# A planned two-MLP attention kernel: four feature tiles of every batch ahead of the other twelve, in new engine orders

## The chip, the core and the metric

The kernel runs on one core of one Trainium2 chip. The metric is the device time of one execution in microseconds (us), the median of three runs. The core's engines are TensorE (PE in the profile; PEld is its weight load), VectorE (DVE), ScalarE (ACT), GpSimd (POOL) and SyncE (SP), whose queue issues nearly all DMA transfers here.

## The reference

Three stages, all in float32. `q`, `k`, `v` have 4 batches of 8 heads, 576 rows, 64 columns.

```python
# Nystrom attention, per batch and head; m = 32 landmarks, each a mean of 18 rows
q_lm, k_lm = q.reshape(B, H, 32, 18, D).mean(3), k.reshape(B, H, 32, 18, D).mean(3)
A, Bm, C = sm(q, k_lm), sm(q_lm, k_lm), sm(q_lm, k)        # sm: softmax of scale * a @ b.T
Z = Bm.T / (norm1(Bm) * norminf(Bm) + 1e-6)
for _ in range(6):
    Z = 2 * Z - Z @ Bm @ Z
x = A @ Z @ C @ v                                          # then (2304, 512)
h = x @ w_in;  x = (h * cos(h)) @ w_out                    # first MLP, 2048 features
h = x @ w_in2; out = (max(h, 0) + alpha * min(h, 0)) @ w_out2   # second MLP
```

The four weights arrive as float64 and are read as pairs of 32-bit words.

## The kernel before

**Products in three passes.** Each operand of a large matmul is split into a rounded part and a rest (`split`, `sub` at L410, the ACT copy at L552 and L1055), and a product is three matmuls: high by high, high by low, low by high.

**Units.** The attention of one batch is two units of four heads (`unit`, L624). The units of batch 0 are u0 and u1 in the order's names, those of batches 1 to 3 are U2 to U7. A unit loads k, q and v (L638, L649, L665), transposes k and q on PE, forms the landmark means (for batches 0 and 1 on PE, L720; for batches 2 and 3 by a tree of additions on POOL, L742), makes the scores (L766), the softmax of C, C by v (L816), and the softmax of A, whose transpose is split into high and low tiles. 

**z path.** `z_path` (L863) runs the iteration for Z. It begins with the products of L882, goes through some fifteen short DVE steps and then through seven products (L936), each waiting for a DVE step (L953) on the one before. Its last product (L965) gives the small matrix `wt`. z0 belongs to batch 0, z1 to batch 1, and z2 to batches 2 and 3 together, in tiles of double width. Only z0 has fillers between its products: matmuls without use, in pairs, named w (L533); ten more pairs open the program.

**V'.** `vprime` (L976) multiplies `wt` by four tiles of the first MLP's input weights (L999, 16 matmul records for 512 features) and splits the result on ACT (L1004) and DVE (L1006). So the first MLP's input product takes A as its moving operand and V' as its weights.

**Ticks.** A tick (`tick`, L1027) is one feature tile of 128 features for one half batch of 288 rows: six matmuls make h (L1043), then ACT, DVE, ACT, DVE, ACT and POOL or DVE form h cos h and split it, and four groups of three matmuls (y, L1068) add it into four PSUM banks. The y groups of a tick stand in PE's order some ticks after its h. There are 128 ticks: first feature tiles 0 to 7 of batches 0 and 1, then 8 to 15 of these, then all 16 of batch 2 and of batch 3. At the end of a block of feature tiles (`e` in the order) the four banks are copied out and stored in `y1d`; a second block of the same half batch reads `y1d` and adds (L1088).

**Weights.** `convert` (L557) loads 512 KB of float64 weights into one of three `raw` tiles (L562) and makes float32 of it by three DVE steps (L568, L570, L572). c0 to c31 are the first MLP's: for each group of 512 features four input tiles, which are also spilled to `w1d` for later batches, and four output tiles. Batches 2 and 3 read their input weights from `w1d` (L983). c32 to c55 are the second MLP's.

**Second MLP.** It is a Strassen product of seven matmul groups (L1357), with the output product at L1438, and runs after the last tick. Its weights and activations take tiles that the first MLP gives up; `place` gives every tag its addresses and an age, and a tile may lie over older ones.

**What sets the order.** `ORDER` is a text of all operations by name, such as `t12:1` (h of tick 12) or `u0:41/V` (the 41st operation of u0, on DVE), and `go` (L327) issues them in that order, each to its engine's in-order queue; without a letter an operation goes to the first engine it names. Due times and `after` lists served a planner that wrote the text; at run time only data dependencies and buffers make an engine wait.

Of the kernel before, what the change touches and what calls it, by code (L numbers as in the profile page):

```python
# [10 lines left out]
F32R = mybir.dt.float32r  # L11
# [21 lines left out]
t3:1 c5:2 U3:16/V t2:4 t1:6 U3:15/A v1:1 t3:2 t0:9 t0:10 t0:8 t2:5 c5:3 t1:7/V c5:4 t3:3 U2:27 t2:6 v1:2 v1:3 U3:10
t0:11 c0:5 c8:5 c1:5 c7:1 c5:5 v1:4 c5:6/V t3:4 U3:11/A U3:12/A v1:5 c6:2 t3:5 U2:28 c12:2 c6:3 t1:9 t4:1 t1:11 U2:23
t5:1 t3:6 t4:2 U2:24/A U2:25/A c6:4 c12:3 t2:7/V t4:3 U2:26 t1:8 t1:10 c6:5 t5:2 t4:4 c6:6/G t5:3 U2:29 U2:30 t4:5
c12:4 t3:7/V t5:4 t4:6 t4:7/G t6:1 t5:5 U2:31 c7:2 U2:32 t7:1 t6:2 t7:2 t5:6 U3:4 U3:5/A t2:9 t2:10 z1:1 t2:8 c7:3
c7:4 U2:33 U2:34/G t7:3 z1:2 z1:3 t6:3 c13:1 c14:1 c9:5 U3:3 c15:1 U3:6/A c7:5 t7:4 t6:4 t5:7/G c7:6/G U3:17 t2:11
U2:35 t7:5 t6:5 U3:19 U3:18 c13:2 U3:20 c13:3 U3:21 U3:22 t8:1 t3:9 t3:10 t3:8 t3:11 t8:2 t6:6 z1:4 t7:6 U2:36 U3:27
U2:37 U3:23 t7:7/G t6:7/G t9:1 c13:4 U2:38 t8:3 z1:5 U3:24/A U3:25/A t8:4 U3:26 z1:6 U2:39/V U3:28 U2:40 z1:7 U3:29
z1:8 U3:7 U2:41 t8:5 z1:9 c12:5 t10:1 U2:42/V U3:8/A c13:5 t9:2 U3:9/A c12:6/V t4:10 z1:17 t4:11 t4:9 t4:8 c14:2  # L40
z1:10 c14:3 t9:3 c13:6/V z1:11 c14:4 t5:9 t5:10 t5:11 t5:8 t9:4 t10:2 t8:6 c14:5 t8:7/G t9:5 z1:12 t10:3 c14:6/V
t11:1 t10:4 t9:6 t9:7/G t11:2 c15:2 z1:13 t10:5 t11:3 z1:14 t6:9 t6:10 t6:11 t12:1 t6:8 t11:4 c15:3 z1:15 t11:5 c15:4
z1:16 t13:1 z1:18 c15:5 t13:2 t12:2 t10:6 U3:30 c15:6/V t13:3 z1:19 U3:31 U3:32 U3:33 t10:7/G U3:34/G t7:8 t7:9 t7:11
z1:20 t7:10 t13:4 t12:3 z1:21 e7:2/A e7:1/A t12:4 e7:4/A U3:35 t11:6 t11:7/G t8:11 z1:22 t12:5 e7:5/V z1:23 e7:3
# [301 lines left out]
def kernel(  # L346
# [1170 lines left out]
```

## Time and profile before

| | us |
|---|---|
| median of three runs | 829.88 |
| lowest and highest | 827.96, 831.62 |
| span of the profiled execution | 827.8 |
| PE busy | 805.2 |
| DVE busy | 610.1 |
| ACT busy | 419.4 |
| POOL busy | 192.9 |

The page gives the profiled execution's span alone; its own time beside it is not shown. In this document a stretch of the trace is bounded by marks of the order: the start of the first h matmul (L1043) of a tick. Tick 0 is at 46.9 us, tick 24 at 128.1, tick 40 at 172.3, tick 64 at 268.1 and tick 127, the last, at 431.1. A gap in which PE stands idle is length less busy time; short waits between pipelined matmuls hide in the busy time.

### The profile page before, as it was taken

What the parts mean: (1) busy time and instruction counts of PE and PEld (TensorE: products, weight loads), DVE (VectorE), ACT (ScalarE), POOL (GpSimd) and SP (SyncE); (2) the same over time, 40 slices, a digit from 0 to 9 for tenths busy, and PEclk for the clock granted to TensorE, in tenths of its full rate; (3) what the DMA queues carried; (4) which work ended last, traced back from release to release, by engine and by line L of the source; (5) the groups of instructions that cost most, each with busy time, mean ns of one, the idle gap of its engine ahead of it and who ended that gap; (6) DMA issues with size and microseconds to landing.
All of it is one profiled execution on the core that took longest, in us unless ns stands there. A gap on an engine that the chain in (4) does not pass through costs nothing.

```text
span 827.8 us, 16875 instructions
## 1 busy us (share of the span) xinstructions
PE 805.2 (97%) x6490; PEld 717.1 (87%) x6490; DVE 610.1 (74%) x1256; ACT 419.4 (51%) x943; POOL 192.9 (23%) x217
## 2 busy tenths in 40 slices
PE   8889999999999999999999999999999999999997
PEld 6567789988788898899999888989998989999886
DVE  3999799877886867889788998765565556456653
ACT  4468655778754557567764444522433244323231
POOL 0003312435530112036621113203400133000020
PEclk9999999999999999999999999999999999999999
DMA  9985466675666864454542422221031012120231
GB/s 222 217 236 155 132 164 209 164 173 115 137 206 210 259 199 151 146 181 168 168 146 87 131 90 66 78 85 39 13 102 51 9 57 83 48 62 14 81 111 26
DMA packets 87904, 103.34 MB, mean 125 GB/s; under 512 B 35856, under 2 KB 62992, under 8 KB 87824
## 3 DMA queue, kind: packets, MB, share of 16 engines
q1 hardware_dynamic: 87744, 102.14, 43.0%
q8 instruction: 51, 0.84, 0.4%
q14 instruction: 29, 0.24, 0.1%
q10 hardware_dynamic: 80, 0.13, 0.0%
HBM read 79.96 MB, written 22.28 MB: 124 GB/s over the span
## 4 chain that ended last, share of the span: by engine, by line
PE 70%; DVE 16%; ACT 5%; DMA 4%; issue 3%; POOL 0%; SPq 0%; DVEq 0%; ACTq 0%; POOLq 0%
PE acc L1438 20%; PE acc L1068 16%; PE h L1357 10%; PE h L1043 8%; PE x L1357 7%; DVE m L410 3%; DVE m L1050 1%; PE x L999 1%; DMA m<-in_moe_w_in_dram 1%; DVE m L572 1%; DVE m L570 1%; DVE m L1053 1%; DMA m<-wi2d 1%; PE x L1402 1%; PE h L1402 1%
## 5 line engine op out<-in xcount | busy, mean ns | idle before, releaser
L410 POOL TENSOR_TENSOR m<-m,m 128x288 fp32r<-128x288 f32 (+4 forms) x154 | 147.1, 968 | 580.0 <-ACT m L1055 213.5
L1068 PE MATMUL acc<-m,m 128*128 128x288 f32 x1536 | 235.4, 299 | 0.1
L1068 PEld LDWEIGHTS acc<-m,m 128*128 128x128 f32 x1536 | 211.2, 188 | 18.7 <-issue 12.7
L1438 PE MATMUL acc<-m,m 128*128 128x512 f32 x864 | 218.0, 392 | 0.6 <-ACT m L1426 0.2
L410 DVE TENSOR_TENSOR m<-m,m 128x512 fp32r<-128x512 f32 (+4 forms) x246 | 151.5, 636 | 48.3 <-ACT m L1426 18.1
L1438 PEld LDWEIGHTS acc<-m,m 128*128 128x128 f32 x864 | 154.1, 188 | 28.4 <-DVE m L410 1.3
L1043 PE MATMUL h<-m,m 128*128 128x288 f32 x768 | 125.0, 302 | 2.5 <-DVE m L1053 1.5
L1043 PEld LDWEIGHTS h<-m,m 128*128 128x128 f32 x768 | 108.5, 190 | 8.3 <-DVE m L1053 4.6
L1357 PE MATMUL h<-m,m 128*128 128x256 f32 x768 | 108.5, 282 | 0.3 <-ACT m L405 0.2
L1357 PEld LDWEIGHTS h<-m,m 128*128 128x128 f32 x768 | 102.6, 189 | 6.3 <-ACT m L405 0.7
L1426 ACT ACTIVATE m<-m 128x512 fp32r<-128x512 f32 (+1 forms) x80 | 46.1, 585 | 92.0 <-DVE m L1424 87.4
L1052 ACT ACTIVATE m<-m,quarter 128x288 f32<-128x288 f32 x128 | 67.0, 533 | 34.5 <-DVE m L1050 33.6
L1357 PE MATMUL x<-m,m 128*128 128x256 f32 x576 | 81.7, 283 | 0.3 <-DVE m L407 0.3
L1357 PEld LDWEIGHTS x<-m,m 128*128 128x128 f32 x576 | 76.5, 189 | 4.2 <-DVE m L407 0.6
L1048 ACT ACTIVATE m<-h 128x288 int32<-128x288 f32 x128 | 51.4, 406 | 47.3 <-PE h L1043 46.4
L405 ACT ACTIVATE m<-h 128x256 f32<-128x256 f32 (+2 forms) x86 | 33.5, 392 | 81.8 <-PE h L1357 65.0
L1050 DVE SCALAR_TENSOR_TENSOR m<-h,m 128x288 f32<-128x288 f32 x128 | 57.0, 450 | 23.8 <-ACT m L1048 23.4
L1055 ACT ACTIVATE m<-m 128x288 fp32r<-128x288 f32 x128 | 55.7, 440 | 30.5 <-DVE m L1053 25.6
L1053 DVE TENSOR_TENSOR m<-m,h 128x288 f32<-128x288 f32 x128 | 56.9, 448 | 12.9 <-ACT m L1052 10.1
L1189 ACT ACTIVATE m<-m 128x512 fp32r<-128x512 f32 x68 | 41.6, 625 | 29.2 <-PE h L1357 10.5
L1380 DVE TENSOR_TENSOR m<-h,m 128x512 f32<-128x512 f32 x32 | 21.9, 686 | 32.8 <-ACT m L405 21.8
L1424 DVE SCALAR_TENSOR_TENSOR m<-m,m 128x512 f32<-128x512 f32 x64 | 45.0, 718 | 0.8
(147 smaller groups left out, 768.0 us busy)
## 6 DMA issues: line engine op xcount, KB each, us to landing
m<-in_moe_w_in_dram SPq DMA_DIRECT2D x32, 512.0 KB, 5.6
m<-wi2d SPq DMA_DIRECT2D x56, 256.0 KB, 3.0
m<-in_moe_w_out_dram SPq DMA_DIRECT2D x24, 512.0 KB, 5.2
m<-w1d SPq DMA_DIRECT2D x32, 256.0 KB, 5.4
y1d<-m SPq DMA_DIRECT2D x24, 288.0 KB, 4.4
out_dram<-m SPq DMA_DIRECT2D x35, 128.0 KB, 2.8
w1d<-m SPq DMA_DIRECT2D x16, 256.0 KB, 5.6
wi2d<-m SPq DMA_DIRECT2D x16, 256.0 KB, 3.2
```

Of the source, the lines that this page charges most:

```text
L410: ENG[e].tensor_tensor(o, a, b, op=ALU.subtract)
L1043: nc.tensor.matmul(out=hp.t[:, 0:CW], lhsT=w_[:, js], rhs=x[:, cs], start=(i == 0), stop=(i == 5))
L1048: op(act(CW, True), lambda e: nc.scalar.activation(k_.t, hp.t[:, 0:CW], AF.Copy, scale=INV2PI, bias=0.25), r=[hp], w=[k_], target=T + 0.8)
L1050: op(dve(CW), lambda e: nc.vector.scalar_tensor_tensor(u.t, hp.t[:, 0:CW], INV2PI, k_.t, op0=ALU.mult, op1=ALU.subtract), r=[hp, k_], w=[u])
L1052: op(act(CW), lambda e: nc.scalar.activation(u.t, u.t, AF.Sin, scale=2.0 * math.pi, bias=quarter), rw=[u], aset="sin")
L1053: op(dve(CW), lambda e: nc.vector.tensor_tensor(hc.t, u.t, hp.t[:, 0:CW], op=ALU.mult), r=[hp, u], w=[hc], target=T + 2.6)
L1055: op(act(CW), lambda e: nc.scalar.activation(gh.t, hc.t, AF.Copy), r=[hc], w=[gh, gl])
L1068: nc.tensor.matmul(out=yg[o].t[:, 0:CW], lhsT=w_.t[:, sl], rhs=x.t, start=(j == ja and i == 0), stop=(j == jb and i == 2),)
L1357: nc.tensor.matmul(out=rv(k), lhsT=a_.t[:, p, c2, js], rhs=b_.t[:, q_, c2, 0:hw], start=(first and c2 == 0 and i == 0), stop=(c2 == 1 and ...
L1424: op(dve(w), lambda e, m_=m_, hv=hv: nc.vector.scalar_tensor_tensor(m_.t[:, 0:w], hv(), 0.0, m_.t[:, 0:w], op0=ALU.max, op1=ALU.add), r=hr ...
L1426: op(act(w), lambda e, m_=m_, gh=gh: nc.scalar.activation(gh.t[:, 0:w], m_.t[:, 0:w], AF.Copy), r=[m_], w=[gh, gl])
L1438: nc.tensor.matmul(out=ya[n][t].t, lhsT=gv(x_), rhs=r_.t, start=(st and k == 0), stop=(en and k == 2))
```

## The change

1. The 128 ticks come in another sequence: feature tiles 0 to 3 of batches 0, 1, 2, 3, then tiles 4 to 15 of each batch. There are 16 blocks in place of 12, and every second block reads `y1d` back.
2. Batches 2 and 3 get a z path each, z2 and z3, in single width.
3. V' of the first 512 features takes the input tiles in place for all four batches (no spill of these); later groups of batches 1 to 3 read `w1d`: 36 reads in place of 32, 12 spills in place of 16.
4. k and q are loaded by transfers over 128 partitions (two heads of 64 groups of nine rows, one above the other) in place of 64; heads take other places in the tiles, and later products follow suit.
5. A tiles of batches 2 and 3, and half of the V' tiles, move to other addresses (`a2`, `a3`, `vb`, `wq`).
6. `ORDER` is new throughout.

```diff
-KN = dict(T0=46, TA=3.4, TBT=3.05, VE=4.0, U1=-1, U2=30, U3=42, UA=88, UD=7, UZ=17, C2=48, CD=3.0, LA=4, JG=8, VG=8, LW=4, LG=4)
+KN = dict(T0=40, TA=3.2, TBT=2.55, VE=4.0, C2=40, CD=3.2, LA=4, VG=10, LW=4, LG=4)
+BLOCKS = [(b, 0, 4) for b in range(4)] + [(b, 4, 16) for b in range(4)]
...
-    at = lay(0, 0, ("f", 4, 4 * FW), ("wo", 8, 2048))
-    at_va = at
+    at_wo = lay(0, 0, ("f", 4, 4 * FW))
+    at_va = lay(0, at_wo, ("wo", 8, 2048))
+    lay(1, at_wo, ("vb", 4, 4096))
+    at = lay(2, at_wo, ("wq", 8, 2048))
...
-    at_1 = lay(1, at_w, ("wp", 24, 2048), ("vb", 4, 4096))
+    at_1 = at_vb + 16384
+    lay(1, at_w, ("wp", 24, 2048), ("a2", 7, 4 * S))
...
+    place["a3"] = (1.5, 4 * S, [z0 + 12288])
...
     def conv_wi(fb, p):
         def done(cf):
             wi1[fb, p] = cf
-            spill((fb, p), w1, w1d[p, :, fb * 512:fb * 512 + 512])(cf)
+            if fb:
+                spill((fb, p), w1, w1d[p, :, fb * 512:fb * 512 + 512])(cf)
...
-                    for bb in range(2):
+                    for hh in range(2):
                         nc.sync.dma_start(
-                            out=t.t[64 * bb:64 * bb + 64].rearrange("p (h x) -> p h x", h=2),
-                            in_=src[b, 4 * c + 2 * bb:4 * c + 2 * bb + 2].rearrange("h (p r) d -> p h (r d)", r=NR),
+                            out=t.t[:, hh * NR * D:(hh + 1) * NR * D],
+                            in_=src[b, 4 * c + 2 * hh:4 * c + 2 * hh + 2].rearrange("b (p r) d -> (b p) (r d)", r=NR),
                         )
...
-                o = loads(4, ld, 3.28, w=[t], after=aft)
+                o = loads(2, ld, 3.28, w=[t], after=aft)
...
-        ah[b, c] = (sb("a", [P, S], F32R), sb("a", [P, S], F32R))
+        ah[b, c] = tuple(sb(("a" if b < 2 else "a3" if b + c + i == 5 else "a2"), [P, S], F32R) for i in range(2))
...
     def vprime(b, fb, target):
-        if b > 1:
+        if b and fb:
...
-    ticks = [(b, ch, j) for jg in range(0, NF, JG) for b in range(2) for ch in range(2) for j in range(jg, jg + JG)]
-    ticks += [(b, ch, j) for b in range(2, NB) for ch in range(2) for j in range(NF)]
+    ticks = [(b, ch, j, ja, jb - 1) for b, ja, jb in BLOCKS for ch in range(2) for j in range(ja, jb)]
...
-        if b != 2:
-            z_path([b] if b < 2 else [2, 3], tick_time(s + KN["UZ"]))
-            gates["v"] = [g.ops[-1]]
+        z_path([b], tick_time(t - 2))
+        gates["v"] = [g.ops[-1]]
...
```

Counted in the two texts of `ORDER`, between the same marks. PE operations of units and z are counted as the order names them; those of the joint z2 are of double size.

| | h | y groups | V' | of units | of z | conversion steps on DVE |
|---|---|---|---|---|---|---|
| before, to tick 0 | 0 | 0 | 1 | 33 | 9 | 19 |
| before, tick 0 to 24 | 24 | 80 | 3 | 13 | 9 | 52 |
| before, tick 24 to 40 | 16 | 64 | 3 | 3 | 0 | 25 |
| before, tick 40 to 64 | 24 | 100 | 2 | 24 | 9 (double) | 15 |
| before, after tick 64 | 64 | 268 | 7 | 1 | 0 | 57 |
| new, to tick 0 | 0 | 0 | 1 | 35 | 10 | 18 |
| new, tick 0 to 24 | 24 | 90 | 3 | 39 | 26 | 20 |
| new, tick 24 to 64 | 40 | 153 | 6 | 0 | 0 | 80 |
| new, after tick 64 | 64 | 269 | 6 | 0 | 0 | 50 |

The order of SP to the first V' was k and q of u0, c3, k and q of u1, c0, v of u0 and u1, c2, c1, then k and q of U2 and more conversions. It becomes k and q of u0, c4, k and q of u1, c2, c3, c1, k and q of U2, v of u0 and u1, q and k of U3, c0, c5, v of U2, c7, c6. Between ticks 24 and 44 the new order issues 18 conversion loads, 9 spills, 7 transfers of `y1d` and 4 reads of `w1d`. The exponent and the sine need different tables on ACT: the order before changes between them 20 times, the new one 12 times, 11 of these before tick 24.

## Rows read from the trace of the kernel before

**Rows 1.** The page: span, and TensorE's busy time and instructions.
```profile
span 827.8 us, 16875 instructions
...
PE 805.2 (97%) x6490; PEld 717.1 (87%) x6490; DVE 610.1 (74%) x1256; ACT 419.4 (51%) x943; POOL 192.9 (23%) x217
```

**Rows 2.** Windows, six stretches between marks (columns in the first line).
```profile
core 0: us, PE busy (x) PEld busy (x) DVE busy (x) ACT busy (x) POOL busy (x), PEclk, DMA share, GB/s
0.00:46.90 46.90, 37.29 (x587) 26.08 (x587) 30.19 (x85) 19.99 (x43) 3.11 (x11) 0.99 0.95 216
46.90:128.10 81.20, 77.16 (x790) 65.56 (x790) 73.22 (x174) 54.39 (x121) 19.35 (x20) 0.98 0.59 170
128.10:172.30 44.20, 44.20 (x355) 40.88 (x355) 39.81 (x78) 30.91 (x73) 18.58 (x20) 1.00 0.70 190
172.30:268.10 95.80, 92.72 (x1056) 79.33 (x1055) 74.90 (x188) 64.53 (x140) 33.13 (x45) 1.00 0.65 166
268.10:431.10 163.00, 162.47 (x1257) 152.88 (x1255) 131.06 (x269) 105.05 (x246) 51.00 (x54) 1.00 0.55 181
431.10:827.90 396.80, 391.36 (x2454) 352.34 (x2454) 260.92 (x467) 144.50 (x321) 67.68 (x68) 1.00 0.21 65
```

**Rows 3.** Chain of waits near 300 us: start, length, what, how many.
```profile
295.46 3.58 PE acc L1068 x27
...
299.04 1.02 PE x L999 x16
...
303.04 1.59 PE h L1043 x12
```

**Rows 4.** Timeline of PE, z path products: one of z0, then z2's.
```profile
38.10 0.43 PE L936 MATMUL h<-m 32*32 32x64 f32 x16 [0.48 <-DVE m L953]
...
235.36 0.46 PE L882 MATMUL x<-m 64*32 64x32 f32 x32
...
255.26 0.87 PE L936 MATMUL x<-m 32*32 32x96 f32 x32
...
259.05 0.67 PE L965 MATMUL x<-m 32*64 32x32 f32 x32
```

**Rows 5.** Timeline of PE: the first V' product.
```profile
41.33 1.33 PE L999 MATMUL x<-m,m 64*32 64x512 f32 x16 [0.60 <-ACT m L731]
```

**Rows 6.** Chain of waits before the first tick: conversion steps, V' copies, tick step.
```profile
19.45 0.43 DVE m L568
...
31.55 0.60 DVE m L570
...
42.68 0.61 ACT m L1004
...
43.31 0.69 DVE m L1006
...
49.83 0.37 DVE m L1050
```

**Rows 7.** Windows before v0 and where transfers are dense (columns as above).
```profile
0.00:41.33 41.33, 33.50 (x558) 24.71 (x558) 25.23 (x77) 17.69 (x38) 3.11 (x11) 1.00 0.98 220
10.00:20.00 10.00, 8.88 (x157) 6.48 (x159) 5.37 (x13) 5.67 (x13) 0.00 (x0) 1.00 1.07 246
50.00:60.00 10.00, 8.00 (x117) 6.12 (x115) 9.42 (x22) 8.29 (x17) 1.07 (x1) 1.00 1.04 263
60.00:70.00 10.00, 9.88 (x107) 8.67 (x108) 9.78 (x24) 6.41 (x18) 2.39 (x2) 1.00 0.65 199
```

**Rows 8.** z0's first and last product (durations in ns, first and last start).
```profile
L882 PE MATMUL h<-m x16: 192/193/214, 19.3 to 19.5; 64*32 64x32 f32 x16
...
L965 PE MATMUL h<-m x8: 217/218/239, 40.3 to 40.5; 32*64 32x32 f32 x8
```

**Rows 9.** Groups of ACT: table loads (count, busy, mean ns, idle before).
```profile
L1052 ACT ACT_TABLE_LOAD x10 | 12.8, 1283 | 0.2
```

**Rows 10.** DMA issues of k: count, size, median us to landing.
```profile
m<-in_k_dram SPq DMA_DIRECT2D x4, 288.0 KB, 5.8
```

More of the change, by code (lines that the diff above doesn't have):

```diff
@@ L762, in unit, with scores @@
                     op([dve2(64), act(64)], kw, r=[lt], w=[kqb[p][i]])
-        def scores(dst, ch, which, t, bb, pp):
+        def scores(dst, ch, which, t, bb, pp, swap=0):
             n = 64 * (CH[ch][1] - CH[ch][0])
             nc.tensor.matmul(
-                out=dst.t[64 * bb:64 * bb + 64, 0:n],
+                out=dst.t[64 * (bb ^ swap):64 * (bb ^ swap) + 64, 0:n],
                 lhsT=kq[pp][:, bb, 2 * which:2 * which + 2].rearrange("p h m -> p (h m)"),
@@ L1027, in tick @@
     def tick(s):
[L1028 removed]
+        b, ch, j, ja, jb = ticks[s]
         T = tick_time(s)
@@ L1130 @@
     n2 = 0
-    US = {KN["U1"]: 1, KN["U2"]: 2, KN["U3"]: 3}
+    first = {}
+    for s, x in enumerate(ticks):
+        first.setdefault((x[0], x[3]), s)
     def attend(b, s):
         gates["ld"] = [h1op[s]] if s >= 0 else gates["ld"]
+        t = first[b, 0]
         for c in range(2):
-            unit(2 * b + c, tick_time(s + KN["UD"] * (c + 1)), tick_time(KN["UA"] + 2 * c) if b == 3 else None)
-        if b != 2:
-            z_path([b] if b < 2 else [2, 3], tick_time(s + KN["UZ"]))
-            gates["v"] = [g.ops[-1]]
-    if KN["U1"] < 0:
-        attend(1, -1)
-        gates["b"].after += [o for o in g.ops if o not in gates["a"].after and any(b.tag and b.tag[0] == "0" for b in o.bufs)]
-        vgroup(1, range(FH))
-    for s in range(NTK):
-        if s == 4 * JG:
-            vgroup(0, range(FH, NFB))
-        if s == 6 * JG:
-            vgroup(1, range(FH, NFB))
-        if s >= 4 * NF and s % (2 * NF) == 0:
-            vgroup(s // (2 * NF), range(NFB))
-        tick(s)
-        if s in US:
-            attend(US[s], s)
-            if US[s] == 1:
-                vgroup(1, range(FH))
+            unit(2 * b + c, tick_time(t - 5 + c), tick_time(t - 2 + c))
+        z_path([b], tick_time(t - 2))
+        gates["v"] = [g.ops[-1]]
+    attend(1, -1)
+    gates["b"].after += [o for o in g.ops if o not in gates["a"].after and any(b.tag and b.tag[0] == "0" for b in o.bufs)]
+    vgroup(1, range(1))
+    for s in range(NTK):
+        b, _, j, ja, jb = ticks[s]
+        if ja and s == first[b, ja]:
+            vgroup(b, range(ja // 4, jb // 4 + 1))
+        tick(s)
+        if s == 0:
+            attend(2, 0)
+            vgroup(2, range(1))
+        if s == 8:
+            attend(3, 8)
+            vgroup(3, range(1))
         while n2 < len(w2) and int(KN["C2"] + KN["CD"] * n2) <= s:
@@ L1163 @@
     for (b, fb), o in vload.items():
-        o.after.append(h1op[max(0, vlast[b - 1 if b > 2 else 0 if fb < FH else 1, fb % FH + FH if b == 2 else fb] - KN["VG"])])
+        o.after.append(h1op[max(0, vfirst[b, fb] - KN["VG"])])
     HF = DFF // 2
@@ L1290 @@
     wo2 = {}
-    gates["o"] = []
+    gates["o"] = [h1op[NTK - 9]]
+    y0ops = [o for o in g.ops if o.key[0] == "y0"]
     def late_wo2(j, target):
@@ L1300, in late_wo2 @@
                     out=raw.t[:, 0:512], in_=w_out2[j * P:(j + 1) * P, 512 * i:512 * i + 512]),
-                0.73, w=[raw, *wo2[j]] if i == 0 else [raw], after=[*gates["o"], h1op[NTK - KN["LG"]]], target=target - 5.0,
+                0.73, w=[raw, *wo2[j]] if i == 0 else [raw], after=[*gates["o"], *y0ops, h1op[NTK - KN["LG"]]], target=target - 5.0,
                 hold=[cf] if i == 0 else [])]
```

512 lines of the change are left out of this document (247 added, 265 removed).

## The prediction

> **What bounds the kernel now.** I read the page first [rows 1]: the span is 827.8 us and TensorE (PE) is busy for 805.2 of it, 97%. So the change can win only what PE loses, and the question is where that lies. The second view cuts the span at marks of the order of work: the first tick (46.9), tick 24 (128.1), tick 40 (172.3), tick 64 (268.1) and the last tick (431.1) [rows 2]. The reader is to subtract busy from length in each row: PE idles 9.6 us before the first tick, 4.0 up to tick 24, 0.0 up to tick 40, 3.1 up to tick 64, 0.5 up to the last tick, 5.4 in the second MLP. DVE is busy 73.2 of the 81.2 us between the first tick and tick 24, over 90%; later it has room. Units U2 and U3 (batch 1) lie in the second row, U4 to U7 (batches 2 and 3) in the fourth.
>
> Idle is not all of the loss, so I price PE's work from a dense place, the chain of waits around 300 us [rows 3]: 12 h matmuls in 1.59 us, so a tick's h (six) is 0.80; 27 y matmuls in 3.58, so a y group (three) is 0.40; one V' product is 1.02. The third stretch tests the prices: 16 h, 64 y, 3 V' and 3 unit operations (0.99 each, below) make 12.8 + 25.6 + 3.1 + 3.0 = 44.5 us against its 44.2.
>
> The two stretches with attention cost more than that. Ticks 40 to 64 hold 24 h, 100 y, 2 V' (61.2 us), 24 PE operations of units, and the nine of the joint z path of batches 2 and 3, each twice the size of a single one: 0.87 against 0.43 [rows 4]. 95.8 - 61.2 - 3.1 idle leaves 31.5; 18 single z at 0.43 are 7.7; so a unit operation costs 0.99, with the small waits that no gap shows. Ticks 0 to 24 hold 24 h, 80 y, 3 V' (54.3), 13 unit operations and 9 z (3.9): 81.2 - 54.3 - 4.0 - 3.9 = 19.0, or 1.46 each. There DVE was the limit: transposes, scores and V' splits stood in its queue behind conversions of weights.
>
> **The change part by part.** PE's instructions are the same ones in another order: 128 ticks, 16 V', 8 units, 17 pairs of fillers; the z path of batches 2 and 3 becomes two paths of single size. I counted both orders between the same marks and price the new one in four pieces, against the profiled span.
>
> *Up to the first tick: 45.9 us.* Ahead of v0:1 the new order has 28 operations of u0 and u1 on PE, as before, and one filler, one z and four unit operations more: 0.5 + 0.4 + 4.0 = 4.9 us. On DVE it has 77 instructions in place of 72, conversions 17 for 16; five in all: four steps of units, two of z, one conversion step of 0.60, less two A steps that go to POOL; I put them at 0.7 us more. Before, v0 started at 41.33 [rows 5], so it comes between 42.0 (the added PE work fits into idle time, of which there are 7.8 us ahead of v0 [rows 7]) and 46.2 (none fits). I take 43.0, as the room is larger than the addition. From v0 to the first tick it took 5.56 us, with a filler, two unit operations of U2 and three conversion steps between. The new order has nothing on PE there and one conversion and one z step on DVE: 1.02 + 0.61 + 0.61 (two ACT copies) + 0.69 [rows 6] = 2.9. That makes 45.9, bounds 44.9 and 49.1. The loads over 128 partitions carry the same bytes in as many or fewer transfers; I take nothing for them. v of u0 and u1 now comes behind about 6.2 and 6.8 MB, not 4.0 and 4.6; at 246 GB/s [rows 7] that is 9 us later, 27 and 29 us with the start, in the middle of z0's chain (19.3 to 40.5 [rows 8]), which needs it only for its last seven products: I leave it inside the bounds.
>
> *First tick to tick 24: 115.4 us.* The new order has 24 h, 90 y, 3 V' (19.2 + 36.0 + 3.1 = 58.3), 39 unit operations and 26 z (11.2). 28 of the 39 are those of U4 to U7, at 0.99: 27.7. The other 11 are of U2 and U3, for which 0.99 and 1.46 are the bounds; I take 1.2, since conversions beside them fall from 52 steps to 20: 13.2. Idle goes with the unit operations, 3.1 for 24, so 5.0 for 39. Sum 115.4; with 0.99 for all and no idle it would be 108.1, with 1.46 for all 133.7 with the idle.
>
> *Tick 24 to 64: 103.7 us.* 40 h, 153 y, 6 V' are 32.0 + 61.2 + 6.1 = 99.3 and nothing else on PE. What is late next are the weights: the eight conversions put off. Between ticks 24 and 44 PE has 20 h, 73 y and 4 V', 49.3 us; DVE has 56 conversion steps (0.43 + 0.60 + 0.60 for three [rows 6], 30.4 us), 49 tick steps at 0.37 (18.1), 12 of 0.60 (7.2): 55.7. So DVE is 6.4 us over, and each conversion sits in front of the tick steps behind it in DVE's queue. After tick 44 it has room again. The cost is between 0 (the lag stays inside the four ticks that y follows h by) and 6.4 from DVE alone; I take 4.5.
>
> *After tick 64: 558.4 us.* Before it was 827.9 - 268.1 = 559.8. The new order has one y more left (0.4), one V' and one unit operation less (1.0 + 0.8). The second MLP has the same operations in a new order; I take its 396.8 us unchanged, give or take its 5.4 of idle.
>
> Costed at nothing: eight more reads and eight more writes of y1d for the 16 block ends in place of 12, and four fewer spills. DMA is at 0.59, 0.70 and 0.55 of its time there [rows 2]; without that cover it would be one landing, some 5 us, at a block end. Third: new places of V' and A tiles. A of batch 3 now ends its life only with the last tick, so one tile of the second MLP's weights waits for it: 0, at most 3.
>
> Sum: 45.9 + 115.4 + 103.7 + 558.4 = 823.4 against the span of 827.8. The median of the three runs, 829.88, is 2.0 above the span (the profiled execution's own time stands nowhere beside it); so 825.4, and I say 825.
>
> At one place the Trainium skill would make it worse. ScalarE swaps its table in 1283 ns, and ACT idles 0.2 us in all before ten such loads [rows 9]. The new order swaps 12 times in place of 20, 11 of them before tick 24: 14 us of ACT. The Trainium skill (ScalarE: Activation LUTs, What ACT_TABLE_LOAD costs) adds a drain of 1.38 us to every swap; by that rule, as an estimate, ACT would have 15 us more in that stretch, and if all of it stood in front of PE the time would be 840. The trace disagrees: 0.2 us in all is not a drain.
>
> **The rivals.**
> *The gain is larger* (811 to 818). With DVE's crowding gone U2 and U3 cost 0.99, the idle stays at 3.1, v0 comes at 42.0 and the conversions hide: -2.3, -1.9, -1.0, -4.5, so 816. For it: 52 conversion steps leave the crowded stretch and DVE there has some 78 us of 115. Against: 39 unit operations in 24 ticks are denser than anything in the trace.
> *Slower: the put-off conversions.* Place: ticks 24 to 44. 18 loads of 0.524 MB, 9 spills and 4 reads of w1d at 0.262, 7 of y1d at 0.295 make 14.9 MB, with only three raw tiles. My 49.3 + 4.5 = 53.8 us asks 277 GB/s. With its engines full (shares of 1.04 and 1.07) the trace moved 263 and 246 GB/s [rows 7], up to the first tick 216 [rows 2]: 56.7, 60.6 or 69.0 us, so 3, 7 or 15 late, 828 to 840. It is slower than before once the rate is under 14.9 / (53.8 + 4.9), 254 GB/s. For it: nearly all loads are needed within three ticks. Against: from 60 to 70 us, where mostly weights are loaded, 199 GB/s took a share of 0.65, which would be 306 at a full one.
> *Slower: the z chains of batches 2 and 3.* Between z2:1 and the V' that waits for it PE has 14 y, 5 unit operations, 1 h and the 9 z, some 15 us. The joint chain took 23.7 us at double size [rows 4], and z0 took 21 [rows 8]. At 21 each, z2's and z3's leave PE 6 us without work, less 3 counted above: +9, 834. It decides from a chain of 15 us on. For it: DVE has over 40 steps in each of these two stretches. Against: z0 stood among more DVE work, 25.2 us of it ahead of v0 [rows 7].
> *No change* (826 to 834): U operations cost 1.46, as in the stretch they most resemble in density, for U2 and U3 alone (+3) and the first tick comes at 49.1 (+3): 831.
> *The new loads run on few engines.* A source of two heads by 64 rows, if carried with the 2 outermost, would go out on 2 of 16 engines: 246 GB/s at 1.07 of 16 is 14 each, 29 for two, so the 1.18 MB of u0's k and q take 41 us, where a k transfer landed in 5.8 [rows 10]: about 860. The two heads lie end to end, so the two dimensions make one of 128. The rule is the Trainium skill's (DMA: Bandwidth & Descriptors, Rules for kernel authors): the outermost dimension sets how many engines serve a transfer. No row of before shows a transfer so confined.
>
> **How the numbers follow.** Forecast 0.43 (its own range 819 to 832), larger gain 0.20, no change 0.14, conversions 0.13, z chains 0.08, loads 0.02. A measurement here tells about 0.5% from no change: below 825.7 is faster, above 834.0 slower. Of the forecast, 0.27 lies below 825.7 and 0.16 between; with the larger gain 0.47 faster. The same: 0.16 + 0.11 of no change + 0.03 of the conversions, 0.30. Slower: 0.23. The range 813 to 837 leaves out the best of the gain and the worst of the three slower cases.
>
> **What would show it.** First tick at 45 to 49 us, tick 24 near 161, tick 64 near 265, the last tick near 425, by starts of the first h matmul. Right if PE's idle between the first tick and tick 24 is about 5 us with DVE under 80% busy there, and DVE is back over 95% around ticks 28 to 44. Conversions as the cause would show as DVE waiting for w_in and w_out loads between 170 and 215 us while PE idles. z chains would show as PE waiting for the subtract after each z product (L953 now). Wrong altogether if PE idles as long before the first tick and the later stretches are dense, or if the second MLP's 396.8 us change by more than 5.

## The result and the profile after

The changed kernel takes 839.46 us (median of 4 runs, 836.14 to 841.96), the kernel before 830.34 in the same job: a ratio of 1.0111, 95% interval 1.0081 to 1.0142. It is slower by some 9 us, and the forecast of 825, its range (813 to 837) included, was wrong. The profiled execution took 836.14 itself, span 834.2; it is the fastest of the four, and three more spans were 836.4, 838.5 and 840.0.

The page after, to be held beside [rows 1]: PE's busy time is the same within 0.5 us, and its idle time grew by some 6.

```profile
span 834.2 us, 16948 instructions
...
PE 805.7 (97%) x6490; PEld 718.1 (86%) x6490; DVE 600.1 (72%) x1283; ACT 393.9 (47%) x894; POOL 258.6 (31%) x270
```

Windows of the changed kernel at the marks tick 0, 24, 44, 64 and 127 (columns as in [rows 2]):

```profile
0.00:49.90 49.90, 39.48 (x674) 28.75 (x674) 29.45 (x87) 20.33 (x48) 10.32 (x17) 1.00 0.84 228
49.90:165.60 115.70, 110.45 (x1334) 87.75 (x1335) 89.00 (x247) 81.83 (x184) 66.06 (x78) 1.00 0.46 120
165.60:226.80 61.20, 55.93 (x406) 47.94 (x404) 56.53 (x120) 36.42 (x86) 13.16 (x12) 0.97 0.74 235
226.80:280.00 53.20, 51.62 (x394) 48.48 (x394) 43.03 (x95) 29.54 (x69) 6.56 (x8) 1.00 0.78 248
280.00:439.40 159.40, 158.46 (x1225) 151.30 (x1225) 115.59 (x246) 94.78 (x227) 55.70 (x62) 1.00 0.55 175
439.40:834.20 394.80, 389.78 (x2465) 353.87 (x2463) 266.51 (x490) 131.03 (x282) 106.81 (x94) 1.00 0.23 69
```

Against the steps of the prediction: 49.9 where 45.9 stood, 115.7 where 115.4 stood, 114.4 (the third and fourth row) where 103.7 stood, and 554.2 where 558.4 stood. The misses are +4.0, +0.3, +10.7 and -4.2, together the 10.8 us between the span and the 823.4 forecast. So two places have to be explained: the stretch ahead of the first tick, and ticks 24 to 64.

**Ahead of the first tick.** The chain of waits (start, length, what) shows DVE, at the very start, on the conversion of c4 while the copies that PE waits for stand behind it, and then a second place near 31 us:

```profile
8.91 0.44 DVE m L564
...
9.37 0.70 DVE m L566
...
11.15 0.57 DVE m L399
...
11.85 0.52 PE h L681 x3
...
30.66 0.17 DVE m L941
...
30.87 0.59 PE h L530 x2
```

The waits of PE in the first 50 us (engine, line, what it waited for; total, times, longest) give the price of both:

```profile
PE h L530 <- DVE m L941: 1.6, 1, 1.6
...
PE h L681 <- DVE m L399: 1.5, 1, 1.5
```

z0 now runs from 21.1 to 47.5 us (first to last start), where it took 19.3 to 40.5 [rows 8]:

```profile
L877 PE MATMUL h<-m x16: 186/193/213, 21.1 to 22.1; 64*32 64x32 f32 x16
```
```profile
L960 PE MATMUL h<-m x8: 217/218/238, 47.3 to 47.5; 32*64 32x32 f32 x8
```

Between its products PE now carries six operations of U2 and U3 of 1.1 to 1.3 us each and a short one (before, three of U2), and the next product stands behind them in PE's queue. The window ahead of v0, to be held beside the first row of [rows 7]:

```profile
0.00:48.15 48.15, 38.39 (x659) 28.57 (x659) 28.26 (x85) 19.70 (x46) 10.32 (x17) 1.00 0.86 235
```

PE is busy there for 38.4 us in place of 33.5, just the 4.9 that the prediction counted, and its idle time didn't shrink but grew from 7.8 to 9.8. That the late v would hold PE up doesn't show: no wait for it stands in the list.

**Ticks 24 to 44.** DVE is busy for 56.5 of 61.2 us, and what is left is largely waiting for loads. The waits there:

```profile
PEld h L1035 <- DVE m L1045: 5.5, 7, 1.5
...
PE h L1035 <- DVE m L1045: 3.2, 5, 1.2
DVE m L564 <- DMA m<-in_moe_w_in_dram: 1.9, 2, 1.3
...
DVE m L564 <- DMA m<-in_moe_w_out_dram: 1.2, 3, 0.7
```

One of these places in the timeline of DVE and then of PE (in brackets the idle time before and what ended it):

```profile
192.58 0.43 DVE L564 TENSOR_SCALAR m<-m 128x512 int32<-128x512 int32 x1 [1.35 <-DMA m<-in_moe_w_in_dram]
192.92 0.81 DVE L1042 SCALAR_TENSOR_TENSOR m<-h,m 128x288 f32<-128x288 f32 x2
194.04 0.46 DVE L1045 TENSOR_TENSOR m<-m,h 128x288 f32<-128x288 f32 x1 [0.31 <-ACT m L1044]
```
```profile
194.56 1.06 PE L1035 MATMUL h<-m,m 128*128 128x288 f32 x6 [1.21 <-DVE m L1045]
```

The two tick steps (L1042) had their inputs from ACT at 190.7 and 191.6, but they stand in DVE's queue behind the first step of a conversion, and that waits 1.35 us for its load. The step that frees the h tile (L1045) is late by that, and there are only two h tiles, so PE stands still for 1.21 us. A late load thus becomes a late tick by way of DVE's queue. Behind this stall PE's granted clock fell to half for some microseconds (windows of 3 us; the third column from the right is the clock, 1.00 being 2.4 GHz and 0.50 being 1.2):

```profile
195.00:198.00 3.00, 2.37 (x26) 1.30 (x25) 3.00 (x7) 0.36 (x2) 0.00 (x0) 1.00 0.53 152
198.00:201.00 3.00, 2.47 (x13) 1.81 (x12) 2.70 (x7) 2.90 (x9) 1.85 (x2) 0.88 0.97 370
201.00:204.00 3.00, 3.00 (x15) 2.96 (x15) 3.00 (x7) 2.74 (x8) 1.68 (x1) 0.55 0.76 226
```

That is 3 x 0.12 + 3 x 0.45 = 1.7 us of matmul time. The spell came behind the stall; that the stall caused it is not shown.

### The profile page after: what moved, and what is told of

The parts are those of the page before. It is cut to its first block, busy times and chain, and to the rows that moved or that the text cites. A ratio compares the mean times of both kernels' runs of the same rounds, so it can differ in the third digit from the quotient of the medians.

```text
span 834.2 us, 16948 instructions
## 1 busy us (share of the span) xinstructions
PE 805.7 (97%) x6490; PEld 718.1 (86%) x6490; DVE 600.1 (72%) x1283; ACT 393.9 (47%) x894; POOL 258.6 (31%) x270
## 4 chain that ended last, share of the span: by engine, by line
PE 78%; DVE 9%; DMA 6%; ACT 4%; issue 2%; POOL 1%; SPq 0%; DVEq 0%; ACTq 0%; POOLq 0%
PE acc L1428 24%; PE acc L1058 17%; PE h L1347 11%; PE x L1347 8%; PE h L1035 8%; DMA m<-in_moe_w_out_dram 3%; DMA m<-in_moe_w_in_dram 2%; DVE m L568 2%; PE x L994 1%; PE h L1392 1%; PE x L1392 1%; PE x L761 1%; DVE m L566 1%; PE x L931 1%; DVE m L1042 1%
## 5 line engine op out<-in xcount | busy, mean ns | idle before, releaser
L402 POOL TENSOR_TENSOR m<-m,m 128x288 fp32r<-128x288 f32 (+4 forms) x200 | 207.1, 1051 | 509.2 <-ACT m L1047 173.3
L1058 PE MATMUL acc<-m,m 128*128 128x288 f32 x1536 | 238.9, 300 | 1.1 <-POOL m L402 0.4
L1058 PEld LDWEIGHTS acc<-m,m 128*128 128x128 f32 x1536 | 212.7, 189 | 19.0 <-issue 8.6
L1428 PE MATMUL acc<-m,m 128*128 128x512 f32 x864 | 210.7, 391 | 0.0
L1428 PEld LDWEIGHTS acc<-m,m 128*128 128x128 f32 x864 | 156.6, 188 | 28.4
L402 DVE TENSOR_TENSOR m<-m,m 128x512 fp32r<-128x512 f32 (+4 forms) x200 | 121.8, 627 | 27.2 <-ACT m L1416 11.4
L1035 PEld LDWEIGHTS h<-m,m 128*128 128x128 f32 x768 | 107.9, 188 | 16.9 <-DVE m L1045 10.1
L1347 PE MATMUL h<-m,m 128*128 128x256 f32 x768 | 105.4, 282 | 0.2 <-ACT m L397 0.2
L1347 PEld LDWEIGHTS h<-m,m 128*128 128x128 f32 x768 | 99.5, 189 | 3.8 <-ACT m L397 0.4
L1045 DVE TENSOR_TENSOR m<-m,h 128x288 f32<-128x288 f32 x128 | 57.4, 450 | 32.9 <-ACT m L1044 26.2
L1042 DVE SCALAR_TENSOR_TENSOR m<-h,m 128x288 f32<-128x288 f32 x128 | 57.6, 451 | 21.0 <-ACT m L1040 20.5
L1047 ACT ACTIVATE m<-m 128x288 fp32r<-128x288 f32 x128 | 55.1, 439 | 28.9 <-DVE m L1045 24.9
L397 ACT ACTIVATE m<-h 128x256 f32<-128x256 f32 (+2 forms) x56 | 21.8, 394 | 65.0 <-PE h L1347 51.3
L397 ACT ACTIVATE m<-x 128x512 f32<-128x512 f32 (+5 forms) x60 | 25.2, 438 | 45.5 <-PE x L1347 26.2
```

Of the source, the lines that this page charges most:

```text
L397: nc.scalar.activation(o, i, AF.Copy)
L402: ENG[e].tensor_tensor(o, a, b, op=ALU.subtract)
L1035: nc.tensor.matmul(out=hp.t[:, 0:CW], lhsT=w_[:, js], rhs=x[:, cs], start=(i == 0), stop=(i == 5))
L1042: op(dve(CW), lambda e: nc.vector.scalar_tensor_tensor(u.t, hp.t[:, 0:CW], INV2PI, k_.t, op0=ALU.mult, op1=ALU.subtract), r=[hp, k_], w=[u])
L1045: op(dve(CW), lambda e: nc.vector.tensor_tensor(hc.t, u.t, hp.t[:, 0:CW], op=ALU.mult), r=[hp, u], w=[hc], target=T + 2.6)
L1047: op(act(CW), lambda e: nc.scalar.activation(gh.t, hc.t, AF.Copy), r=[hc], w=[gh, gl])
```

## The experiments

The stretches of every kernel that has the new order, in us, from its own profile; the ratio to the kernel before stands where there are several runs. Each row of stretches is one profile.

| | to tick 0 | 0 to 24 | 24 to 44 | 44 to 64 | 64 to 127 | time | ratio (95%) |
|---|---|---|---|---|---|---|---|
| changed kernel | 49.9 | 115.7 | 61.2 | 53.2 | 159.4 | 839.46 | 1.0111 (1.0081 to 1.0142) |
| pool_low | 51.4 | 115.8 | 64.2 | 53.7 | 159.7 | 843.2 | 1.0164 (1.0142 to 1.0187) |
| skip_step | 54.1 | 116.4 | 58.9 | 52.8 | 159.5 | 838.25 | 1.0099 (1.0074 to 1.0125) |
| half_load | 52.5 | 115.8 | 57.8 | 52.5 | 159.7 | 834.97 | 1.0068 (1.0042 to 1.0094) |
| skip_half | 49.5 | 115.7 | 55.0 | 53.2 | 159.4 | 831.01 | one run |
| almost_none | 54.1 | 115.2 | 53.7 | 51.7 | 159.9 | 832.68 | one run |
| early_six | 54.0 | 126.5 | 55.9 | 52.2 | 159.4 | 846.05 | 1.0196 (1.0180 to 1.0212) |
| prologue | 47.0 | 116.1 | 63.6 | 55.1 | 159.9 | 838.62 | 1.0109 (1.0089 to 1.0129) |
| prologue_c4_alone | 48.9 | 116.4 | 62.7 | 54.6 | 159.6 | 839.57 | one run |
| early_prologue | 47.2 | 125.4 | 54.7 | 53.4 | 160.5 | 840.04 | 1.0131 (1.0114 to 1.0148) |

Seven of these profiles (all but the three named for the prologue) have the same work ahead of the first tick, and still it came between 49.5 and 54.1. The difference is the clock. Windows of 4 us, the changed kernel and then skip_step:

```profile
28.00:32.00 4.00, 2.37 (x94) 1.64 (x86) 2.82 (x12) 0.46 (x2) 1.41 (x2) 1.00 1.16 228
32.00:36.00 4.00, 3.52 (x70) 2.82 (x68) 2.40 (x7) 1.65 (x3) 0.86 (x1) 1.00 0.30 113
36.00:40.00 4.00, 4.00 (x120) 3.35 (x116) 2.55 (x5) 1.23 (x3) 1.16 (x1) 1.00 0.78 197
```
```profile
28.00:32.00 4.00, 2.39 (x67) 1.53 (x66) 2.86 (x13) 0.51 (x2) 1.38 (x2) 0.83 1.14 222
32.00:36.00 4.00, 3.99 (x64) 2.97 (x60) 0.28 (x1) 1.56 (x3) 0.90 (x1) 0.50 0.34 116
36.00:40.00 4.00, 3.53 (x40) 3.10 (x42) 3.21 (x7) 0.10 (x1) 1.16 (x1) 0.50 0.24 63
```

In both, PE is busy for about 2.4 of the 4 us up to 32, where it waits for z0:18. In skip_step the clock then falls to half for some 10 us. Two of the seven (49.9 and 49.5) kept the full clock and five did not (51.4 to 54.1). prologue_c4_alone has the same wait for z0:18, 1.6 us, and kept the full clock too, so the wait alone does not decide it. The other three runs of the changed kernel had spans 2.2 to 5.8 us longer than its profiled one. For the longest the mean granted clock accounts for that (0.989 where the profiled one had 0.996, and 0.007 of 834 is 5.8 us); the other two had 0.995, worth some 0.8 of their 2.2 and 4.3 us, and the rest is open.

**before_loads128.** Part 4 of the change alone, in the kernel before:

```diff
-                    for bb in range(2):
-                        for hh in range(2):
...
-                o = loads(4, ld, 3.28, w=[t], after=aft)
+                    for hh in range(2):
...
+                o = loads(2, ld, 3.28, w=[t], after=aft)
```

> The kernel before with the one part of the change that loads k and q over 128 partitions (with the places of heads that follow from it), its order of work untouched. In the changed kernel u0's k was there for ACT at 4.6 us, before at 6.0. Theory: the first tick comes 0.5 to 1.5 us earlier than 46.9 and the whole is 0 to 1.5 us shorter, 829 to 830. Rival: the new loads cost something that the new order hides or adds to its lateness: the first tick comes later than 47.5 us and the whole is 2 to 4 us longer.

828.74 us against 829.46, ratio 0.9994 (0.9979 to 1.0008). The first tick came at 45.6 in place of 46.9, but tick 8 at 73.8 in place of 72.8. So the new loads, tried in the order before, are no cause of the loss; what they gain is gone eight ticks later.

**pool_low.**

```diff
-... t26:7/V ... c12:6/V ...
+... t26:7/G ... c12:6/G ...
```

> The changed kernel with 31 subtractions of ticks 24 to 64 (23 tick steps, 8 of weights) issued to POOL in place of DVE. In the changed kernel ticks 24 to 44 took 61.2 us, with DVE busy for 56.5 of it and POOL for 13.2. Theory DVE (its queue is what bounds that stretch): 8.6 us of DVE work leave it, so it takes 53 to 55 us, ticks 44 to 64 take about 51 in place of 53.2, and the whole comes to 831 to 833. Rival DMA (the loads bound it): the stretch stays at 60 or more, the whole at 838 to 840. Rival POOL: its step is 1.05 us in place of 0.45, y waits for it, and the stretch becomes longer than 61.

It became slower, 64.2 us in ticks 24 to 44, as rival POOL had it, but not by y's waits alone. Groups of DVE there, first the changed kernel, then this one, where the same three conversion steps are seven lines further down (L571, L573, L575):

```profile
L568 DVE SCALAR_TENSOR_TENSOR m<-m,m 128x512 int32<-128x512 int32 x20 | 13.4, 684 | 0.0
L566 DVE SCALAR_TENSOR_TENSOR m<-m,m 128x512 int32<-128x512 int32 x19 | 13.1, 698 | 0.0
...
L564 DVE TENSOR_SCALAR m<-m 128x512 int32<-128x512 int32 x20 | 8.4, 424 | 3.0 <-DMA m<-in_moe_w_in_dram 1.9 <-DMA m<-in_moe_w_out_dram 1.2
```
```profile
L573 DVE SCALAR_TENSOR_TENSOR m<-m,m 128x512 int32<-128x512 int32 x19 | 14.8, 789 | 0.1
L575 DVE SCALAR_TENSOR_TENSOR m<-m,m 128x512 int32<-128x512 int32 x20 | 14.0, 714 | 0.0
L571 DVE TENSOR_SCALAR m<-m 128x512 int32<-128x512 int32 x20 | 10.6, 534 | 4.8 <-DMA m<-in_moe_w_out_dram 3.0 <-DMA m<-in_moe_w_in_dram 1.9
```

15 subtractions, 7.7 us of DVE, went over to POOL, and 4.5 us came back in conversion steps that grew longer (14.8 + 14.0 + 10.6 against 13.4 + 13.1 + 8.4). DVE's theory was not tested by this run as meant, since DVE's busy time (in which steps overlap) fell only from 56.5 to 54.8 us; and the clock, at 0.95 in the stretch, took 3.2 us, where the changed kernel lost 1.7.

**skip_step, half_load, skip_half, almost_none.** Cuts of DVE's work, of the bytes, of both, and of nearly all:

```diff
+        n = 512 if 12 <= len(cvops) < 32 else 1024      # half_load, skip_half; 64 in almost_none
...
-            ... out=raw.t[:, 0:1024], in_=w[r * P:(r + 1) * P, 2 * c0:2 * c0 + 1024]),
+            ... out=raw.t[:, 0:n], in_=w[r * P:(r + 1) * P, 2 * c0:2 * c0 + n]),
...
+        skip = 12 <= len(cvops) - 1 < 32                # skip_step, skip_half, almost_none (there the third step too)
-        op(dve(512), lambda e: nc.vector.scalar_tensor_tensor(
+        op(dve(512), lambda e: None if skip else nc.vector.scalar_tensor_tensor(
```

> The changed kernel without the second of the three DVE steps in conversions c12 to c31 (values wrong, loads and all else kept): some 18 steps of 0.69 us less between ticks 24 and 44. Theory DVE: the stretch falls from 61.2 to 50 to 52 us, near PE's own 49.3, and the whole to 828 to 831. Rival DMA: the raw tiles come free earlier but the bytes are the same, the stretch stays at 59 or more and DVE's waits for loads grow by as much as its work falls; the whole 837 or more.

> The changed kernel with half the columns loaded in conversions c12 to c31 (values wrong, DVE's steps all kept): 4.7 MB less between ticks 24 and 44. Theory DVE: only DVE's 3.1 us of waiting for loads can go, the stretch takes 58 to 60 us in place of 61.2, the whole 836 to 838. Rival DMA: the stretch falls to 52 to 54 us and the whole to 831.

> The changed kernel with both cuts at once in conversions c12 to c31: no second DVE step and half the columns loaded (values wrong). Alone they took the stretch from tick 24 to 44 from 61.2 to 58.9 and 57.8 us, with DVE busy for 48.1 and 55.8 of it. Theory of two limits: DVE and the loads each hold it at about the same length, so either cut alone uncovers the other, and both together bring 50 to 52 us, near PE's own 49.3. Rival, the tick's own chain: with two PSUM tiles for h and five steps on ACT and DVE a tick can't go faster in this order, and the stretch stays at 56 or more.

> The changed kernel with hardly any conversion work left in c12 to c31: one DVE step of three, and 64 of 1024 columns loaded (values wrong). With one step and half the columns cut, ticks 24 to 44 took 55.0 us, 5.7 over PE's own 49.3. Theory, all of the excess is conversions: DVE's work there falls to some 35 us, and the stretch takes 49 to 51 us. Rival, this order's own waits (h tiles, V' products between ticks): it stays at 54 to 55.

Windows from tick 24 to 44, in this order:

```profile
170.50:229.40 58.90, 54.35 (x404) 46.40 (x404) 48.10 (x103) 35.90 (x87) 11.56 (x12) 1.00 0.77 246
```
```profile
168.30:226.10 57.80, 54.29 (x404) 46.34 (x403) 55.82 (x120) 36.17 (x86) 12.86 (x12) 1.00 0.54 172
```
```profile
165.20:220.20 55.00, 53.19 (x405) 46.29 (x404) 46.67 (x103) 36.00 (x87) 11.84 (x12) 1.00 0.57 183
```
```profile
169.30:223.00 53.70, 52.00 (x405) 46.14 (x404) 36.35 (x84) 35.71 (x87) 11.56 (x12) 1.00 0.42 130
```

Neither theory held alone. With a step less, DVE is down to 48.1 us, but the loads stay at 246 GB/s, DVE's waits for them grow from 3.1 to 4.9 us, and the stretch falls by only 2.3; with half the columns the loads have room (share 0.54), but DVE stays at 55.8 of 57.8 us. Both together bring 6.2. All four have the full clock, so the changed kernel's 1.7 us of half clock are among these gains. One caution: from tick 24 to 64 the changed kernel, prologue and prologue_c4_alone have the same order, and their profiles took 61.2, 63.6 and 62.7 us in ticks 24 to 44. Against that spread of 2.4 the gain of one cut alone is little or not resolved (the intervals of both whole times overlap the changed kernel's), while 6.2 and 7.5 stand clear of it. The theory of two limits stands, its number doesn't: 55.0, not 50 to 52. almost_none shows why. With DVE down to 36 us and the DMA share to 0.42 the stretch still takes 53.7, as that run's rival had it: of the 11.9 us over PE's dense price 4.4 are left. They are at most this order's own, since almost_none keeps one step of every conversion. PE's idle time fell from 5.3 to 1.7 us and its busy time from 55.9 to 52.0, so most of the 4.4 lies in busy time beyond the dense price. In ticks 44 to 64 it takes 51.7 in place of 53.2. What makes up the 4.4 was not taken further apart.

**early_six, prologue, prologue_c4_alone, early_prologue.**

```diff
-... u0:5 c4:3 u1:1 u1:2 c2:1 c4:4 u0:21 u0:11 u0:7 u0:8 u0:6/V ...
+... u0:5 u1:1 u1:2 c2:1 u0:21 u0:11 u0:7 u0:8 u0:6/V c4:2 c4:3 c4:4 ...
-... z0:15 u1:39 z0:16 u1:29 ... u0:45 z0:17 z0:18 u1:31 ...
+... z0:15 u1:39 z0:16 z0:17 z0:18 u1:29 ... u0:45 u1:31 ...
-... c0:4 c5:1 z0:27 ...
+... c5:1 z0:27 c0:4 ...
```

The first pair is prologue_c4_alone, all three are prologue. early_six has none of these, but 36 moves like the two below (six steps of six conversions, the last of them on POOL); early_prologue has both sets.

```diff
+    place["rx"] = (1, 4096, [at])
-        raw = sb("raw", [P, RAW], I32)
+        raw = sb("rx", [P, 1024], I32) if len(cvops) in (12, 13, 14, 15, 20, 21) else sb("raw", [P, RAW], I32)
-... U4:10 c10:1 z1:21 ... U3:37 U4:12/V z1:22 ...
+... U4:10 c10:1 c12:1 z1:21 ... U3:37 U4:12/V c12:2 z1:22 ...
```

> The changed kernel with six of the conversions of output weights (c12 to c15, c20, c21) moved ahead, into ticks 4 to 21, over a raw tile of their own of 4 KB in memory that is free until then; their loads fall into 58 to 135 us, where the DMA share was 0.11 to 0.65. Theory: some 11 us of DVE work and 3.1 MB leave ticks 24 to 44, which take 50 to 53 us in place of 61.2; tick 0 to 24 takes 116 to 118; the whole 830 to 833. Rival: the attention of batches 2 and 3 pays for it, since DVE's queue carries its softmax and z steps: tick 0 to 24 takes 122 or more and the whole stays at 838.

> The changed kernel with three moves in its order ahead of the first tick: the DVE steps of c4 behind the copies of u0's transposes, z0's first product and the DVE step behind it (z0:17, z0:18) ahead of u0's and u1's softmax steps, the last DVE step of c0 behind z0:27. In the changed kernel the first tick came at 49.9, and in three more profiles with the same prologue at 51.4, 52.5 and 54.1, with PE's clock granted at half in some of 31 to 41 us, behind a wait of 1.6 us for z0:18. Theory: the wait and the half clock go, the first tick comes at 46 to 48.5 us, the whole at 834 to 836. Rival: the 4.9 us of PE work that the new order puts ahead of v0 set the first tick; it stays at 49.5 or later, and the whole at 838 or more.

> The changed kernel with one of the three moves ahead of the first tick: the DVE steps of c4 behind the copies of u0's transposes. With all three the first tick came at 47.0. Theory: PE's wait of 1.5 us near 11.8 goes, the wait for z0:18 near 31 us stays and with it the chance of the half clock: first tick 48 to 48.5, or 50 to 53 with it. Rival: that wait near 11.8 was slack and nothing moves: 49.5 or more without any half clock.

> The changed kernel with the six early conversions and the three moves ahead of the first tick. If both theories hold, the first tick at 46 to 48.5, ticks 24 to 44 in 50 to 53 us, and the whole at 825 to 829, at or below the kernel before; if the attention of batches 2 and 3 pays for the conversions, 833 or more.

The three moves do what was expected ahead of the first tick: 47.0 and 47.2, without the half clock, and 48.9 with the first of them alone. The lead holds to tick 24 (163.1 against 165.6). But the whole, 838.62, was only 0.8 below the changed kernel, and the ratios are alike: ticks 24 to 64 took 118.7 us in place of 114.4. The profile has two spells of half clock there (206 to 212 and 238 to 242 us, 1.7 us each) behind stalls of PE of 2.5 and 2.0 us, one spell more than the changed kernel's. The rest is mostly idle time: PE stands idle for 10.0 us in these ticks, 6.9 in the changed kernel. The longest stall is a V' product that waits for the conversion of its weights, where the changed kernel waited 0.95:

```profile
207.15 1.69 PE L994 MATMUL x<-m,m 64*32 64x512 f32 x16 [2.52 <-DVE m L568]
```

From tick 24 on this is the changed kernel's order, and prologue_c4_alone, with 117.3, has it as well; so one order spreads over 4.3 us here. Whether an earlier start adds to it is not shown.

early_six shortened ticks 24 to 44 to 55.9 us, where almost_none took 53.7. It paid for that between ticks 8 and 24, first the changed kernel, then this one:

```profile
84.10:165.60 81.50, 77.57 (x930) 62.09 (x930) 61.97 (x173) 55.95 (x129) 48.25 (x60) 1.00 0.53 142
```
```profile
88.30:180.50 92.20, 80.29 (x931) 63.72 (x930) 74.97 (x188) 59.44 (x135) 58.35 (x67) 0.98 0.55 148
```

DVE had 19.5 us free there, its busy time rose by 13.0, and the stretch grew by 10.7. A spell of half clock (0.98) is 1.7 of that; between prologue and early_prologue, both at full clock there, the growth is 9.3 (82.0 to 91.3). POOL is busy for 10.1 us more as well, and how much of the cost goes by way of POOL was not separated. PE now waits for the copies and scores of the units, which stand behind the conversions:

```profile
PE x L704 <- ACT m L397: 3.0, 2, 2.8
PE x L762 <- DVE m L399: 2.7, 2, 1.5
PE x L794 <- ACT m L786: 1.4, 1, 1.4
```

So the rival was right, and early_prologue, with both, ends at 840.04.

**before_v0_first.**

```diff
-... u1:46/V v0:3 u1:47 v0:5 c9:3 u1:48 U2:10 c9:4 u1:49/V ... U2:17 c10:1 c4:1 t0:1 ...
+... u1:46/V u1:47 v0:3 u1:48 v0:5 u1:49/V U2:10 t0:1 t0:2 t0:3 c9:3 c9:4 ... U2:17 c10:1 c4:1 ...
```

> The kernel before with k and q loaded over 128 partitions and eleven tokens moved around its first V': the last A steps of u1 and V's splits ahead of two conversion steps on DVE, h of tick 0 ahead of the scores of U2 on PE. With the loads alone the first tick came at 45.6 us, the half clock took some 2 us between 48 and 56, and the whole was the same. Theory: the first tick comes at 44 to 45, the spell of half clock shrinks, the whole at 826 to 828. Rival: DVE, busy for over 90% up to tick 24, sets that stretch whatever comes first: tick 24 stays at 128 and the whole at 829.

830.56 against 830.56, ratio 1.0001 (0.9992 to 1.0010), as the rival had it. The first tick came at 43.3, 3.6 us earlier than before, and nothing of it is left at tick 8 (74.1 against 72.8). Within eight ticks 4.9 us were lost. The half clock took 2.7 of them on the spot:

```profile
48.00:52.00 4.00, 1.11 (x8) 0.84 (x8) 3.84 (x9) 3.40 (x8) 0.00 (x0) 0.83 1.07 257
52.00:56.00 4.00, 3.98 (x44) 3.58 (x46) 3.10 (x7) 2.30 (x5) 1.07 (x1) 0.50 0.95 280
```

That is 4 x 0.17 + 4 x 0.50, and 0.7 more falls between 56 and 60 us (0.82). But the kernel before loses 1.7 us to a spell of its own between 46 and 50 (0.53 and 0.62 in windows of 2 us), so the clock explains some 1.7 of the 4.9. From 48 to 52 us PE was busy for 1.1 of 4 us and DVE for 3.8. No version here beats the kernel before.

## Why the prediction was wrong, point by point

*Up to the first tick, 45.9 (44.9 to 49.1): wrong.* The step that failed is "I take 43.0, as the room is larger than the addition". v0 came at 48.2, past the upper bound of 46.2, at which none of the added PE work fits into idle time. The 4.9 us of added work came as counted, but it did not fill waits: PE's idle time ahead of v0 grew by 1.9. Some 3 us of the work stood between z0's products (PE is busy for 21.1 us in that chain, 18.2 before), and the chain itself became longer, 26.4 us in place of 21.2. And one change of the order was not priced at all, c4's steps ahead of the first copies (1.5 us of PE's waiting; its move brought the first tick to 48.9). The run-to-run half clock, up to 4.6 us, was not in any bound. From v0 to the first tick, 2.9 was forecast and 1.8 measured.

*First tick to tick 24, 115.4: right,* 115.7, with 5.25 us of idle for 5.0 and DVE at 77% (89.0 us, where *the gain is larger* had some 78; and 32 conversion steps leave that stretch, not 52). The upper sum there, with 1.46 for all, comes to 131.4 and not 133.7, which changes nothing. The late v and the z chains of batches 2 and 3 cost nothing that shows: PE's waits for the subtract after z products are 1.0 us in ticks 8 to 24. So *the gain is larger* and *z chains* both fall.

*Ticks 24 to 64, 103.7: wrong,* and the largest miss. The term that failed is the 4.5 us for the put-off conversions. Held against almost_none they cost 7.5 in ticks 24 to 44 and 1.5 after it, 9.0 in all (one profile of each, with the spread given above). The bound of 6.4 "from DVE alone" was no bound. It took DVE's work as the whole of what can be late, but DVE was also idle for 4.7 us, 3.1 of them waiting for loads, with tick steps queued behind; and 1.7 us of half clock came behind the stalls. The other term that failed is the 99.3 under it: almost_none took 53.7 + 51.7, 6.1 more. The dense prices came from one place of the chain [rows 3]. For ticks 64 to 127 of the kernel before (63 h, 252 y, 7 V', 1 unit operation) they give 159.3 us against the 162.9 that these took, so they are some 2% low, about 2 of the 6.1; the rest stays open. Of the signs, DVE's waits for w_in and w_out loads came (3.1 us); the marks came late (165.6, 280.0, 439.4), and DVE was busy for 92% of ticks 28 to 44, not over 95%.

*The rival of the put-off conversions: right in place and size, half right in cause.* Its 60.6 us for ticks 24 to 44, at 246 GB/s, is close to 61.2, and the loads moved 235. But half the bytes alone gave back 3.4 us, not the 7 that it charged to the rate. I had weighed DVE and the loads as two cases, of which one would hold; they hold together.

*No change:* its 49.1 for the first tick was near the 49.9 of this profile, its +3 for the unit operations did not come. *The new loads:* not confined to few engines. k of u0 and u1 lands in a median of 4.9 us, where it took 5.8 [rows 10], far from that rival's 41. So the rule of the Trainium skill (DMA: Bandwidth & Descriptors, Rules for kernel authors), by which the outermost dimension sets how many engines serve a transfer, does not bite here. *The table swaps:* ACT idles 0.7 us in all before the eleven loads after the start, so the agreement of its 840 with the time is chance.

*After tick 64, 558.4: 554.2 measured.* Ticks 64 to 127 took 2.2 us less than forecast and the rest 2.0 less, inside the 5 I had allowed; almost every variant has 159.4 to 159.9 there and 394.8 to 396.2 after it.

## What to carry to other kernels

Work that is put off into a dense stretch is to be priced against every resource it uses there at once: in-order queues couple them, so a transfer that is 1.3 us late holds up everything behind the step that waits for it, even where neither resource is full by itself. Free time of an engine inside a chain of dependent steps is not room for other work: conversions that took 13 of 19.5 us of DVE's free time, and 10 of POOL's, cost 10.7. And an earlier first tick is worth only what the next stretch lets through: in the kernel before, 3.6 us were gone after eight ticks.

## What the runs showed of the hardware

Stalls of PE of 1.2 to 2.5 us were often followed by a second cost: in several profiles the granted clock fell from 2.4 to 1.2 GHz behind them, for 1.7 us of matmul time a spell in ticks 24 to 64 and for 2 to 4.6 us ahead of the first tick. Stalls of the same length without it stand beside these: the one of 1.6 us ahead of the first tick had it in five of eight profiles. So one order can spread by several microseconds between runs, and what decides is not shown.

Moving work from DVE to POOL lengthened single DVE steps. The durations (min/median/max in ns) of a conversion step in ticks 24 to 44, then of a tick step that reads PSUM, of pool_low:

```profile
L573 DVE SCALAR_TENSOR_TENSOR m<-m,m x19: 678/684/1296, 169.1 to 228.4; 128x512 int32<-128x512 int32 x19
```
```profile
L1049 DVE SCALAR_TENSOR_TENSOR m<-h,m x20: 444/450/458, 168.7 to 231.2; 128x288 f32<-128x288 f32 x20
```

The median of the first is what it was (685 in the changed kernel), but its longest went from 930 to 1296, that of L575 from 691 to 1049 and that of L571 from 467 to 1041, while the step with one operand in PSUM never moved. So a few steps were stopped, rather than all slowed. All twelve conversion steps that took over 10% longer than their median ran beside a POOL instruction; nine of the twenty steps at L1049 did so too and took no longer. The Trainium skill (SBUF — State Buffer, Who interferes with whom) says that the two engines share a port pair under an exclusive lock: a DVE step with two inputs in SBUF contends with a POOL step that reads SBUF, and one with at most one such input does not, outside the 2-port modes. The steps at L573 and L575 (two inputs in SBUF) and at L1049 (one) agree. L571 has one and was stopped as well, which the rule covers only if that step runs in a 2-port mode; no run here shows that.
